# A transformer block on one core: new landing times, gates and priorities for the planner that orders its instructions

## The chip, the core and the metric

The kernel runs on one core of a Trainium2 chip. The core has five engines that each run their own instruction stream in order: TensorE (PE, matrix products; its weight loads are shown apart, as PEld), VectorE (DVE), ScalarE (ACT), GpSimd (POOL) and SyncE (SP, which here only issues DMA transfers). They wait for each other by semaphores. The metric is the device time of one execution in microseconds (us).

## What is computed

A block with 2048 rows of width 448: adaptive layer norm, a segment-wise attention with a compressive memory, adaptive layer norm, a gated FFN. Cut to what matters:

```python
mod = (silu(c) @ w_mod).reshape(1, 6, 1, 448)
sa, ca, ga, sb, cb, gb = (mod[:, i] for i in range(6))
h = layernorm(x) * (1 + ca) + sa
x = x + ga * A(h)            # attention
h = layernorm(x) * (1 + cb) + sb
x = x + gb * B(h)            # FFN: (sigmoid(h @ w_gate) * (h @ w_up)) @ w_down
# A: 16 heads of 28, 4 segments of 512 rows, in each segment s:
logits = q_s @ k_s.T * scale + causal mask
a_dot = softmax(logits) @ v_s
a_mem = (phi(q_s) @ M) / (phi(q_s) @ z + 1e-6)
o_s = g * a_mem + (1 - g) * a_dot     # g = sigmoid(beta), a number for each head
M, z = M + phi(k_s).T @ v_s, z + phi(k_s).sum()   # phi(t) = t + 1 if t > 0 else exp(t)
# then o @ wo
```

## The kernel before

The work is cut into four segments of 512 rows (four tiles of 128). A segment goes through these steps, each a function in the code:

- `ln1`: statistics (L607, L608) and scaling (L620, DVE, result xn), the power for the standard deviation on POOL (L614, L615), then turning to hT, features on partitions. Segments 0 to 2 turn in PE with an identity (`turned`, L821), segment 3 by a DMA transpose (`transposed`, L766, on SP). The turned tiles are scaled and shifted by the modulation columns `cols` while they are copied out of PSUM (L841 on DVE, L843 on ACT).
- `proj`: q, k and v (L881, L893) and their copies (L864, L866). The heads are taken in four groups; the weights wq and wk are first copied into a padded tile wqk (L696, the pads `W_p`).
- `attention`: logits (L962), exponential (L976, L982), causal mask (L989 on POOL, L992 on DVE), product with v (L1017), the memory's part (L1032), and a normalisation with 32 x 32 transposes on DVE (L1044 to L1069).
- `memory`: the update of M, with a DMA transpose pk (L917) and a product (L925).
- `wo_ln2`: output projection (L1084), residual (L1087), the second norm. Here the turning is by DMA transposes for all segments, and two DMA exchanges between the partition halves follow (`modulated`, L783 and L786).
- `ffn`: gate and up products (L1106), tanh (L1111), their product (L1113), the down projection (L1125), residual (L1132) and the store (L1134).

The modulation columns of the first norm come from two blocks of 32 small products (`mod_cols`, L659), which need w_mod, loaded in two halves into the tile pT by ACT's and SP's queues (`load_wm`). Each block is copied to `cols` (L671, L669). Warm-up products on zeros (L703) fill PE before the first data.

None of this is issued in program order. Each step adds a node to a graph, with a duration for each engine that may run it, dependences, buffers, a lag and a priority. `Graph.run` simulates the graph and fixes each engine's order for good: at each point of planned time an engine takes, among its ready nodes, the one with the highest rank plus priority. The rank is the length of the longest chain behind the node, in ns. The priorities come from the lists in PRM by kind of work and segment (`pr`), except for the prologue, which has fixed ones in units of BIG = 1e7. `COST` weighs the engines against each other where a node may run on several; `STAY` is a bonus for staying in one mode of PE. Where the plan leaves PE free for 465 ns or more, `fillers` puts in products on the identity (L1149), one for each 215 ns. The chip then runs this order, and waits wherever the plan was too hopeful.

A transfer's planned landing is the end of its bytes on a modelled link, plus 800 ns, plus its own lag. The lag is 300 for a load unless given, LATE for the first w_mod load. The bytes of a queue go at 215 per ns when it is alone and 111 when the other queue is busy too:

```python
a = max(self.ring[e], t)
b = self.ring["ACT" if e == "SP" else "SP"]
both = min(max(b - a, 0.0), size / SHARED)
self.ring[e] = a + both + (size - both * SHARED) / ALONE
```

Loads are kept from piling up: from load number UNTIED on, each waits for the third load ahead of it (`tie = loads[-DEPTH]`, L478 issues them). The loads in order are x tiles 0 and 1, c, x tiles 2 and 3, two halves of w_mod, wq, wk, x of segment 1 in two, wv in two, and then all others.

The fixed priorities of the prologue: turning of segment 0 and copies out, 2 BIG; modulation blocks, 1.5 BIG; pads, BIG.

Of the kernel before, what the change touches and what calls it, by code (L numbers as in the profile page):

```python
# [25 lines left out]
    "ld": (651902, 891758, 992046, 193839, 837972, 665983, 316786, 476619, 43274, 343803, 286986, 160628, 711024,  # L26
        773136, 92427, 200204, 1044173, 736930, 1243772, 692528, 937636, 616944, 1210630, 537419, 680585, -894676,
        101351, 728950, 607455, 1023026, 727687, 781942, 744416, 1320064, 1621173, 1242993, 1028480, 145604),
    "ws": (-134299, -217321, -175544, -243931, 15607, -528928, -1120744, 499755, -1822165, -1211957, -825377, -739006,
        -1049662, -916501, -1040707, -866299, -901616, -1444816),  # L30
    "pj": (2135341, 1765591, 2105194, 1672348, 1755362, 2254245, 1789709, 1512327, 2053089, 2138977, 2019869, 1835313,
        1733495, 1561732, 1467880, 1624953, 2164447, 1911795, 2076941, 1474725, 1071842, 2337649, 857487, 1479601,
        340869, -293016, -359807, -247015, -176478, -354654, -81637, -1181532, -1278023, -1553286, -1474034, -1392027,
        -2227875, -2649473, 738263, -485647, 458907, 1008596, 310603, 72906, -72493),
    "ev": (-294718, -287247, 213078, 345921, 516457, 617525, 581324, 337607, 190516, 201212, 1078717, 752663, -206309,
        -398653, -811894, 100457, 154660, -509455, -370130, -33664, 711493, 754309, 1092631, 1295115, 103302, -75744,
        -184717, 157515, -78688, 1103999, -567928, -409370, -842817, 129441, -1343027, -1834626, -1457093, -912663,
        -759990, -1105822, -1876991, -2484939, -1306058, -1489059, -1970976, -2040367, -2466205, -1875557),
    "ln1": (110333, -435438, 43989, 509127, 558340, 18640, -99722, 403841, 461985, -125721, 570633, 547192, 181038,
        589914, 838716, 388754, 1549344, 884134, 773881, 472463, 684753, 1450874, 1288325, -324762, -757540, 462703,  # L40
        235067, -196974, -90708, 130840, -2467, 24163, -173465, 12535, 560453, 321271, 141093, -574140, 352985,
        535548, -27157, 188824, 69165, 444536, -98687, 179524, -418944, -519050, -477785, -435607, 170856, 3212,
        -130603, 225709, -490768, -1222499, -1370121, -708993, -934798, -2273487, -922214, -1803841, -1194051,
        -1317455, -631182),
    "lg": (1930058, 1751837, 2089657, 1566292, 1503804, 777354, 1687163, 1461078, 820009, 478679, -574235, 441736,
        833992, 1205983, 71857, -209236, 98120, 699703, -386863, -451811, 1247966, 1710428, 1838855, 1608378, 1427664,
        1416671, 1472264, 1000048, 1902810, 635876, 2045809, 2348474, 1639360, 1253914, 1989642, 1870767, 1290318,
        1369680, 1105828, 441201),
    "ex": (820874, 1464092, 742402, 1721040, 1588269, 1846081, 2243894, 1771657, 1278231, 1694284, 1696793, 1148671,
        1565931, 874544, 290916, 2057927, 1431436, 2197370, 1532130, 1893428, 1169769, 1278223, 1429592, 1653293,  # L50
        1950929, 2335322, 1322958, 1489306, 651480, 1429262, -822129, -568907, -867507, -821319, -915357, -596973,
        -1379940, 58334, -1027319, -1394623),
    "mask": (871790, 1336268, 1642602, 1644196, 1580291, 1182991, 674167, 1522842, 1002934, 1339526, 1073208, 582064,
        806458, -167410, 381420, 458481, 768451, 1021063, 768364, 1088419, 901901, -33154, 1426954, 633166, 1054260,
        1617974, 575398, 1050025, 603812, 1402523, 831035, 1969148, -693227, -381531, 32884, 993657, 1101369, 762326,
        770126, 972849, 917495, 580251, 1626792, 824996, 833044, 991639, 1289478, 1708424, 1923893, 200297, 1240980,
        2126685, 1325623, 360160, 807428, 463327, 872714, 1369800, 930140, 1251419, 959998, 1315368, 1685662,
        1707343),
    "pv": (915183, 562989, -255863, 207624, -948513, -1784647, -1359691, -1851218, -448878, -576520, -1377485,
        -1039085, 451562, 1234285, 626677, 1171067),  # L60
    "t": (1504447, 1142971, 1498285, 249197, 2006853, 932728, 1830786, 1496977, 1797028, 1067225, 1669551, 1012448,
        1493008, 245545, 653293, 1730310, 1032521, 637393, 578213, 475817, 1194895, 670368, 1005069, 539542, 266975,
        1086409, 757943, -119979, 184266, 68176, 1299326, 1062841, 604854, 457056, 1415477, 944850, 1237728, 1143919,
        1252723, 678851, 1173350, 1767221, 1154668, 1170984, 1681291, 1120494, 1331949, 1053049, 114568, -116665,
        371052, 1074348, 157535, -270325, 57161, 181528, 155732, 83145, 820449, -137672, 478795, 592777, 337533,
        433694, -202781, -202925, -14119, -255487, 286501, -610255, -386903, -587025, -682549, -752560, -331807,
        -514855, 2993984, 2444729, 2526547, 2592569, 1889775, 2716625, 2740846, 2238225, 3066811, 2555029, 2940307,
        2968972, 3148894, 2939222, 3361905, 3605619, 3121992, 2896025, 3786564, 3061300, 4197354, 3108144, 3332194,
        2584841, 3453168, 2446031, 3115253, 2130779),
    "mem": (632660, 14836, 625612, 169379, -203457, 219971, 3166, -112832, -111979, 400067, 34302, -305861, -473627,  # L70
        724682, 1011534, 7776, -63822, -68838, -464677, 74183, -156399, -503372, 638892, 144364, 142364, 963326,
        143123, 722786, -135667, -577822, -742004, -540413, -835757, -207903, -673805, -93199, -145891, -144444,
        -1396541, -396310, -711511, -1297484, -612133, -706851, -521833, -164102, -1061841, -381836, -535280, -768057,
        -430175, -185845, -301056, -257799, -994564, -326051, 482086, -300754, 239236, -952235, 494754, -511897,
        -79917, -1085942, -464958, -54359, -490405, -912243, -220855, -554793, -1096452, -558009, -125262, -737088,
        -493049, 283968, -306712, -164819, -867118, -745049, -658321, -1182633, -704357, -75582),
    "wo": (-61225, -75610, -121003, -877351, 538559, 801450, 680069, 475534, 1947394, 2116079, 1713439, 2519473,
        1964361, 2559016, 1811544, 1942394),
    "ln2": (1346281, 1522029, 2339337, 1896659, 1268025, 1827698, 1561458, 2411495, 2740913, 2397362, 2049726,
        1098393, 2056240, 1643426, 1469752, 1516714, 1503039, 1478138, 884620, 2154157, 536839, 1153782, 1227142,  # L80
        1747539, 996154, 665586, 897788, 2523183, 1944058, 2236027, 1719000, 2079467, 2506460, 3182459, 1815723,
        2991530, 2290986, 2230887, 2272823, 2833817, 1237511, 2266504, 1938033, 2625708, 2553773, 1994448, 2041106,
        2451926, 2874528, 2571820, 2619831, 2092098, 966660, 1097378, 1524106, 456777, 1624191, 588984, 45196,
        1118750, 557760, -281000, 1006893, 656336, 1046263, 431849, 954219, 585672, 353355, -238055, 107673, 50010,
        345968, 893779, -98119, 643221, 921020, 288029, -1423125, -1558137, -1804997, -1640448, -1713062, -1930084,
        -1748829, -1453154, -1463181, -1412064, -2530358, -2348000, -2087770, -2284133, -2265972, -2613909, -2444750,
        -2567702, -2676544, -3771402, -2534665, -3238719, -1971814, -3299744, -2935510, -3033738),
    "gu": (354734, -15197, 452284, 727077, -177490, 490389, 991533, 1098033, 722194, 573386, 345008, -153917, 637103,
        553581, 563006, 683739, 596089, 885873, 850342, 930801, 510761, 1699749, 1022095, 1497866, 1021360, 753752,
# [23 lines left out]
        -742516, -2205172, -701131, -944493, -341370, -1186633, -855811, -1182823, -459652, -1152001, -584859),  # L113
}
STAY = 96324
COST = {"ACT": 0.957, "DVE": 0.883, "POOL": 0.756}


class Slot:
# [225 lines left out]
def kernel(  # L345
# [24 lines left out]
    NK = 4  # L370
# [100 lines left out]
    BIG = 1e7  # L471
# [36 lines left out]
    def first(i):  # L508
        return 5 * BIG - i * 1e6
# [673 lines left out]
```

## Time and profile before

| | us |
|---|---|
| median of 3 runs (lowest, highest) | 264.01 (263.14, 265.35) |
| profiled execution | 263.85 |
| its span, first to last instruction | 262.1 |
| PE busy in the span, fillers included | 245.5 |
| fillers (L1149) alone | 11.1 |
| DVE busy | 198.3 |
| ACT busy | 152.5 |
| POOL busy | 43.1 |

A span begins with the first instruction and ends with the last; the time of the execution has something around it. An engine's busy time is the sum of its instructions, so a PE that is busy may be busy with fillers, or at half clock: the mean granted clock of PE is 0.987 of full speed. A line of the timeline has the start, the duration of the instructions that were merged into it, engine and line of the code, the tiles, the number of instructions, and in brackets how long the engine was idle before and what ended that.

### The profile page before, as it was taken

How to read it: one execution, taken by the hardware profiler on the slowest of the kernel's cores; microseconds unless marked ns; L12 is line 12 of the kernel's file. 1: busy time of each engine (PE TensorE's matmuls, PEld its weight loads, DVE VectorE, ACT ScalarE, POOL GpSimd, SP SyncE). 2: the span in 40 equal slices, each digit the busy share in tenths (PEclk: the TensorE clock that was granted, in tenths of full speed). 3: DMA queues.
4: the chain of work that ended last, by engine and by line, in shares of the span. 5: the costliest groups of instructions: out<-in, count | busy, mean ns of one | idle time of the engine just before them, and what ended most of it. 6: DMA issues, size and time to landing. Idle time of an engine off the chain costs nothing.

```text
span 262.1 us, 6080 instructions
## 1 busy us (share of the span) xinstructions
PE 245.5 (94%) x2424; PEld 111.9 (43%) x2424; DVE 198.3 (76%) x497; ACT 152.5 (58%) x189; POOL 43.1 (16%) x99
## 2 busy tenths in 40 slices
PE   8799999789978999998999999999999999999994
PEld 3464545443333544443544344444344344454442
DVE  4749999987999999989499969898699754333431
ACT  5026989889987887663597745779730231122300
POOL 5205310010640224400000000503002200000000
PEclk9769999999999999999999999999999999999999
DMA  5975778997253200553111200132100420110011
GB/s 142 203 174 135 193 208 191 165 216 198 41 85 90 41 34 0 42 105 67 22 23 42 54 18 3 21 63 77 48 0 18 83 70 3 36 35 3 0 38 35
DMA packets 30088, 19.79 MB, mean 75 GB/s; under 512 B 18603, under 2 KB 28524, under 8 KB 30060
## 3 DMA queue, kind: packets, MB, share of 16 engines
q1 hardware_dynamic: 29532, 18.77, 32.8%
q10 hardware_dynamic: 528, 0.63, 0.9%
q8 instruction: 19, 0.31, 0.5%
q14 instruction: 9, 0.07, 0.1%
HBM read 11.07 MB, written 1.84 MB: 49 GB/s over the span
## 4 chain that ended last, share of the span: by engine, by line
PE 44%; DVE 29%; DMA 19%; issue 3%; ACT 2%; SPq 1%; POOL 1%; DVEq 0%; POOLq 0%; ACTq 0%
PE ps L1106 26%; PE ps L1125 10%; DMA wgu<-in_B_w_up_dram 4%; DMA pT<-in_w_mod_dram 3%; DVE x_sb L1087 3%; DVE st L607 3%; DMA hT<-hT 3%; DVE fT L1113 2%; DVE pT L992 2%; DMA fT<-in_w_mod_dram 2%; DVE A L1044 2%; PE ps L881 2%; DVE U L1059 2%; PE ps L1017 2%; PE ps L821 2%
## 5 line engine op out<-in xcount | busy, mean ns | idle before, releaser
L1106 PE MATMUL ps<-hT,wgu 64*128 64x512 bf16 x784 | 92.9, 377 | 2.6 <-DMA hT<-hT 1.4
L1111 ACT ACTIVATE tt<-ps 128x512 f32<-128x512 f32 x56 | 33.4, 596 | 60.5 <-PE ps L1106 54.4
L976 ACT ACTIVATE pT<-ps 128x2048 bf16<-128x2048 f32 x32 | 60.3, 1883 | 9.2 <-PE ps L962 8.7
L1106 PEld LDWEIGHTS <-wgu 64*128 64x128 bf16 x784 | 39.7, 94 | 49.3 <-issue 13.3
L1113 DVE SCALAR_TENSOR_TENSOR fT<-tt,ps 128x512 bf16<-128x512 f32 x56 | 37.9, 680 | 27.1 <-ACT tt L1111 27.1
L1125 PE MATMUL ps<-wd_sb,fT 128*128 128x448 bf16 x224 | 46.4, 354 | 0.2 <-DVE ot L1132 0.2
L1125 PEld LDWEIGHTS <-fT 128*128 128x128 bf16 x224 | 20.2, 98 | 22.8 <-issue 6.1
L881 PE MATMUL ps<-hT,wqk 64*128 64x512 bf16 x224 | 27.2, 377 | 0.3 <-DVE qT L866 0.3
L607 DVE BATCH_NORM_STATS2 st<-x_sb 128x6 f32<-128x448 bf16 x32 | 19.8, 618 | 3.1 <-DMA x_sb<-in_A_x_dram 2.8
L989 POOL TENSOR_SCALAR_AFFINE_SELECT pT<-pT 128x512 bf16<-128x512 bf16 x19 | 11.9, 636 | 58.3 <-ACT pT L976 28.9
L614 POOL TENSOR_SCALAR rs<-mv 128x1 f32<-128x1 f32 (+1 forms) x29 | 6.5, 225 | 81.3 <-DVE mv L608 52.8
L992 DVE TENSOR_TENSOR pT<-pT,cmask 128x512 bf16<-128x512 bf16 x45 | 17.4, 417 | 2.9 <-ACT pT L976 2.1
L615 POOL TENSOR_TENSOR rs<-rs,mhalf 128x1 f32<-128x1 f32 (+1 forms) x29 | 17.2, 594 | 2.4
L1132 DVE TENSOR_TENSOR ot<-ps,x_sb 128x448 bf16<-128x448 f32 x16 | 9.8, 617 | 9.0 <-PE ps L1125 8.7
L881 PEld LDWEIGHTS <-wqk 64*128 64x128 bf16 x224 | 11.0, 94 | 13.1 <-issue 2.2
L962 PE MATMUL ps<-qT,kT 28*128 28x512 bf16 (+3 forms) x256 | 15.9, 300 | 0.7 <-ACT pT L976 0.5
L982 ACT ACTIVATE pT<-ps 128x2048 bf16<-128x2048 f32 x8 | 15.1, 1881 | 1.6 <-PE ps L962 1.5
L1084 PE MATMUL ps<-wo_sb,oT 128*128 128x448 bf16 x64 | 13.5, 354 | 0.4 <-DVE oT L1069 0.4
L620 DVE TENSOR_SCALAR xn<-x_sb,mv,rs 128x448 bf16<-128x448 bf16 x32 | 11.4, 387 | 2.5 <-POOL rs L615 2.5
L1017 PE MATMUL ps<-pT,vt 128*32 128x512 bf16 (+3 forms) x256 | 11.4, 301 | 1.2 <-DVE pT L992 0.9
L893 PE MATMUL ps<-wvv,hT 64*128 64x448 bf16 x112 | 11.3, 350 | 0.0
L843 ACT ACTIVATE hT<-ps,cols 128x512 bf16<-128x512 bf16 x5 | 4.0, 800 | 12.3 <-DVE cols L669 10.9
(96 smaller groups left out, 260.1 us busy)
## 6 DMA issues: line engine op xcount, KB each, us to landing
out_dram<-ot SPq DMA_DIRECT2D x16, 112.0 KB, 1.7
fT<-in_w_mod_dram SPq DMA_DIRECT2D x8, 196.0 KB, 2.8
wgu<-in_B_w_gate_dram SPq DMA_DIRECT2D x7, 224.0 KB, 3.3
wgu<-in_B_w_up_dram SPq DMA_DIRECT2D x7, 224.0 KB, 3.6
wd_sb<-in_B_w_down_dram SPq DMA_DIRECT2D x7, 224.0 KB, 2.8
x_sb<-in_A_x_dram SPq DMA_DIRECT2D x6, 224.0 KB, 3.8
hT<-hT SPq DMA_DIRECT2D x5, 256.0 KB, 3.2
hT<-hT SPq DMA_DIRECT2D x5, 192.0 KB
```

The source lines that it names most:

```text
L607: nc.vector.bn_stats(st_r[:, st.at, :], src)
L615: nc.gpsimd.tensor_tensor(r, r, mhalf[:, 0:w], ALU.pow)
L881: nc.tensor.matmul(pf(b), lhsT=w, rhs=piece(hT, i, half), start=(i == 0), stop=(i == NP - 1))
L962: nc.tensor.matmul(ps[:, lg.at + hs, o:o + nq], lhsT=kT_r[r, k.at, hcs[u], kb * P:(kb + 1) * P], rhs=qT_r[r, q.at, hcs[u], kb * P:L], star ...
L976: nc.scalar.activation(pT_r[:, pTs[units[0]].at, :, w0:w0 + L], ps_, AF.Exp, scale=scale)
L982: nc.scalar.activation(dst, ps_.rearrange("p h (u w) -> p u h w", u=2), AF.Exp, scale=scale)
L992: nc.vector.tensor_tensor(blk, blk, cmask[:].rearrange("p (o k) -> p o k", o=1).to_broadcast([P, 4, P]), ALU.mult)
L1017: nc.tensor.matmul(pf(acc)[hs * HP:(hs + 1) * HP, kb * P:L], lhsT=vt_r[:, v.at, kb, hc * 4 + hs, :], rhs=pT_r[:, pT.at, hs, OFF[kb]:OFF[kb ...
L1106: nc.tensor.matmul(pf(b), lhsT=wgu[half * HR:(half + 1) * HR, chunk_of(i, half), fs], rhs=piece(hT, i, half), start=(i == 0), stop=(i == N ...
L1111: a = act(485, lambda gp=gp, tt=tt: nc.scalar.activation(tt_r[:, tt.at, :], pf(gp), AF.Tanh, scale=0.5), [n], use=[gp, tt], prio=pr("tanh" ...
L1113: f = dve(597, lambda up=up, tt=tt, ft=ft: nc.vector.scalar_tensor_tensor(fT_r[:, ft.at, :], tt_r[:, tt.at, :], 1.0, pf(up), op0=ALU.add, ...
L1125: nc.tensor.matmul(pf(b)[:, 0:D], lhsT=fT_r[:, fts[fc].at, t * P:(t + 1) * P], rhs=wd_sb[:, fc, :], start=(fc == 0), stop=(fc == NFC - 1))
```

## The change

Five things are changed, all in what the planner is told; no instruction is added or removed apart from fillers.

1. All priorities in PRM, and STAY and COST, have new values.
2. LATE, the lag of the first w_mod load, is 2200 instead of 500. wq and wk have lags of 1900 and 1200 instead of 900 each.
3. UNTIED is 13 instead of 9.
4. The pads of head group 0 have priority 2.5 BIG; the other groups keep BIG.
5. DMA transposes have a lag of 400 instead of 0; the two exchanges 900 and 1000 instead of 400 and 500.

```diff
-    "lg": (1930058, 1751837, 2089657, 1566292, 1503804, 777354, 1687163, 1461078, 820009, 478679, -574235, 441736,
...
+    "lg": (3531987, 2928887, 3302070, 2312646, 1981257, 2222351, 1556422, 2079865, 2540545, 1674238, 496386, 1265056,
...
-STAY = 96324
-COST = {"ACT": 0.957, "DVE": 0.883, "POOL": 0.756}
+STAY = 69838
+COST = {"ACT": 0.956, "DVE": 0.949, "POOL": 0.819}
...
-    EARLY, LATE = -900, 500
-    DEPTH, UNTIED = 3, 9
+    EARLY, LATE = -900, 2200
+    DEPTH, UNTIED = 3, 13
...
-    W_qk = [load_half("SP", wqk_st, half, w, first(6 + half), lag=900) for half, w in enumerate((A_wq, A_wk))]
+    W_qk = [load_half("SP", wqk_st, half, w, first(6 + half), lag=1900 - 700 * half) for half, w in enumerate((A_wq, A_wk))]
...
-            W_p.append(add(("DVE", "ACT", "POOL"), (415, 838, 830), pad, [W_qk[half], n_pads, n_th, *ln0], prio=BIG, lock=True))
+            W_p.append(add(("DVE", "ACT", "POOL"), (415, 838, 830), pad, [W_qk[half], n_pads, n_th, *ln0], prio=BIG if h else 2.5 * BIG, lock=True))
...
-        return add("SP", 1305, fn, [n], use=[xn, hT], prio=prio, move=60000)
+        return add("SP", 1305, fn, [n], use=[xn, hT], prio=prio, move=60000, lag=400)
...
-        xs = [add("SP", 530, below, hs[0:NK - 1], use=[hT], prio=prio(), move=80000, lag=400),
-              add("SP", 600, above, hs, use=[hT], prio=prio(), move=80000, lag=500)]
+        xs = [add("SP", 530, below, hs[0:NK - 1], use=[hT], prio=prio(), move=80000, lag=900),
+              add("SP", 600, above, hs, use=[hT], prio=prio(), move=80000, lag=1000)]
...
-                pk_r[:, pk.at, :, :], pq_r[:, f2.at, :]), [n], take=[pk], use=[f2], move=60000, prio=pr("mem", s))
+                pk_r[:, pk.at, :, :], pq_r[:, f2.at, :]), [n], take=[pk], use=[f2], move=60000, lag=400, prio=pr("mem", s))
```

The lists in PRM run over the segments; for the kinds that the prediction names, the mean of the quarter that belongs to a segment (millions, before and after):

| kind | segment 0 | segment 1 | segment 2 | segment 3 |
|---|---|---|---|---|
| lg, logits | 1.41, 2.41 | 0.17, 0.71 | 1.43, 0.90 | 1.54, 0.71 |
| t, normalisation | 1.07, 1.54 | 0.88, 0.24 | 0.16, 0.86 | 2.94, -0.69 |
| wo | -0.28, 1.80 | 0.62, 1.46 | 2.07, 0.47 | 2.07, 0.05 |
| ln2 | 1.60, 1.46 | 2.26, 1.01 | 0.60, -1.42 | -2.26, 2.51 |
| gu, gate and up | 0.48, 2.44 | 0.97, 0.44 | 0.62, 0.40 | 0.24, 0.71 |

## The prediction

> **What bounds the kernel now.** I read first the busy time in stretches of 20 us, then the prologue in the timeline, then the clock, then what TensorE (PE) waited for. Columns of the stretches: length, busy time of PE, its weight loads, VectorE (DVE), ScalarE (ACT), POOL, granted clock, DMA share, GB/s.
>
> ```profile
> 0.00:20.00 20.00, 16.84 (x135) 9.10 (x137) 10.92 (x36) 5.32 (x13) 5.25 (x23) 0.83 0.80 174
> 20.00:40.00 20.00, 19.46 (x232) 9.29 (x231) 19.12 (x57) 16.86 (x22) 7.45 (x18) 1.00 0.68 178
> 40.00:60.00 20.00, 17.55 (x268) 8.52 (x270) 17.80 (x57) 17.54 (x22) 1.28 (x2) 1.00 0.99 194
> 60.00:80.00 20.00, 17.23 (x168) 6.91 (x164) 18.31 (x47) 18.19 (x18) 7.61 (x14) 1.00 0.48 100
> 80.00:100.00 20.00, 19.53 (x219) 9.01 (x220) 19.48 (x48) 15.44 (x17) 4.58 (x7) 1.00 0.19 48
> ```
>
> PE looks full, but part of it is filler (L1149). The same stretches for that line alone, columns PE and weight loads:
>
> ```profile
> 0.00:20.00 20.00, 3.91 (x15) 1.45 (x15) 0.83 0.80 174
> 60.00:80.00 20.00, 4.75 (x18) 1.51 (x18) 1.00 0.48 100
> 80.00:100.00 20.00, 1.64 (x6) 0.50 (x6) 1.00 0.19 48
> ```
>
> So PE has three regimes. Up to 20 us it does almost nothing that counts; from 40 to 100 us it is starved (idle 2.45 + 2.77 + 0.47, fillers 4.75 + 1.64: 12.1 us), because DVE (89 to 97% busy) and ACT (77 to 91%) feed it; after 100 us it is the bound, idle 7.1 us in 162. The FFN's first product (L1106) starts only at 80.9 us. The prologue, in the timeline:
>
> ```profile
> 7.57 0.70 DVE L620 TENSOR_SCALAR xn<-x_sb,mv,rs 128x448 bf16<-128x448 bf16 x2
> 8.73 0.70 DVE L620 TENSOR_SCALAR xn<-x_sb,mv,rs 128x448 bf16<-128x448 bf16 x2 [0.46 <-POOL rs L615]
> 10.00 1.51 PE L659 MATMUL ps<-silu,pT 112*128 112x32 bf16 x32 [1.88 <-DMA pT<-in_w_mod_dram]
> 11.35 4.16 PE L821 MATMUL ps<-ident,xn 128*128 128x128 bf16 x32
> 15.30 1.30 PE L659 MATMUL ps<-silu,pT 112*128 112x32 bf16 x32
> 16.44 3.53 PE L1149 MATMUL ps<-ident 128*128 128x512 bf16 x14
> 16.84 2.35 DVE L841 TENSOR_SCALAR hT<-ps,cols 128x512 bf16<-128x512 bf16 x5
> 19.91 3.20 PE L881 MATMUL ps<-hT,wqk 64*128 64x512 bf16 x28
> ```
>
> The normalised tiles are there at 8.3 and 9.4 us, PE is free at 8.1, yet the 32 transposes (L821) stand behind the first modulation columns (L659), which wait for w_mod until 10.3; the second columns stand behind the transposes, and the first projection behind all of it, at 19.9. The clock is halved meanwhile (column after POOL):
>
> ```profile
> 8.00:10.00 2.00, 0.12 (x1) 0.00 (x1) 1.41 (x4) 0.00 (x0) 0.61 (x2) 1.00 1.13 201
> 12.00:14.00 2.00, 2.00 (x18) 1.38 (x16) 1.35 (x9) 0.00 (x0) 0.00 (x0) 0.50 0.96 208
> 16.00:18.00 2.00, 2.00 (x25) 1.05 (x22) 1.32 (x4) 0.78 (x1) 0.00 (x0) 0.70 0.97 214
> ```
>
> **The change: the order in the prologue.** LATE 500 to 2200 moves the planned landing of w_mod. By the code's own link arithmetic (start 2000, 215 or 111 bytes per ns, +800, +lag) its second half lands at 7.4 us planned before and at 9.1 after; the first tile's transposes are ready at about 7.5. I use the plan only for order: before, columns first; after, all four tiles first (2e7 outranks 1.5e7). On the chip: PE free at 8.13; tile 0 (8.13 to 8.62), tile 1 to 9.11, tile 2 when its xn is done (9.08, plus 0.1) to 9.67, tile 3 to 10.16. I took 61 ns for a transpose, from the later group that took 1.96 us for 32 at clock 1.00. The columns then start when w_mod is there, 10.29. Before, the first block's successor started 1.06 us after 10.29, and from the second block's start to the first hT copy were 1.54 us (15.30 to 16.84). So second block at 11.35, first copy at 12.89: **3.95 us earlier**.
>
> [...] In the trace it fell at 10.4, 2.2 us after the last dense product; by this row the moved transposes still run at full clock. If they were cold from the start, 32 would take the 4.16 us of the row, 8.13 to 12.29, and the first copy would be at 12.29 + 1.06 + 1.54 = 14.9: gain 1.95. I take 3.95, since the clock row at 8 to 10 us shows 1.00, and 1.9 as the other end.
>
> **The pads, and the loads behind them.** Pad copies of head group 0 (L696) get 2.5e7 and go ahead of the hT copies. wq landed before 12.1 (four pads ran at 12.12); wk, by when SP's tied issue went on, about 13.8. With lags 1900 and 1200 the plan puts the k pad behind the first hT copy; on DVE it then waits from 13.4 to 13.8 and takes 0.37, and four hT copies stand behind it, ACT taking the other two or three. Copies ended 2.8 us after their start before (16.84 to 19.62); after: 12.89 + 2.8 + 0.8 = 16.5 against 19.6. Without cover, each us that wk is late is a us for the copies. Projection of groups 0 and 1 is 28 instructions in 3.20 us; group 0 goes chunk by chunk behind the copies and ends near 16.9, group 1 near 18.5, against 23.1: gain 4.6. With the clock halved until 17.2 (as now) it ends near 19.3: 3.8; halved throughout, 20.0: 3.1. Fewer fillers (about 6 by the new gap instead of 14) make that end possible.
>
> UNTIED 13 lets four more loads go untied: x of segment 1 (two, 0.4 us of issue each) and wv (two, 0.61 and 1.33). On SP they pass its waits for w_mod (6.1 us), wq (0.9) and wk (1.7), and are issued from about 4 to 7 us; nothing else is on SP until the transposes at 40 us, POOL's queue issues none, and ACT's load isn't passed. They stand behind wk on the same queue, so wk shouldn't suffer; the hole in DMA at 14 to 16 us (53 GB/s there) goes, about 1.4 us of the load stream. wv landed 6.9 us after issue at 14.55, about 21.4; its product starts at 26.8, so it stays covered at 23.
>
> I take **3.5** for the prologue (ends 1.9 and 4.6).
>
> **Does it carry?** DVE is 45% idle before 20 us and nearly full behind it, and what feeds PE up to 80.9 is DVE and ACT work that can start 3.5 us sooner. Then it reaches the end: the last copy starts 3.3 us before the end and that is fixed.
>
> **The later landings.** Lags of 400 on DMA transposes and 900 and 1000 on exchanges put planned landings at 2.8 and 2.6 us or so, where the trace has 3.4 (pk), 2.9 and 3.2. What PE lost to these:
>
> ```profile
> PE ps L925 <- DMA pk<-pq: 2.9, 4, 1.0
> PE ps L659 <- DMA pT<-in_w_mod_dram: 1.9, 1, 1.9
> PE ps L1106 <- DMA hT<-hT: 1.4, 2, 0.9
> ```
>
> At most 4.3 us; at the pk waits PE is starved anyhow, so I count 0 (0 to 2).
>
> **All priorities, COST and STAY are new**, so everything behind the prologue is reordered too. No row prices this. From above: half the 12.1 us of holes (6). From below: 8 us, worked out under the rivals. I take 0: total work is unchanged and both old and new plans fill PE by the same rules.
>
> Sum: 262.1 - 3.5 = 258.6 us of span; the profiled execution took 263.85, 1.75 more than its span, so 260.35; it lay 0.16 under the median: **260.5 us**.
>
> **Rivals.**
> 1. *Load stream binds (no change).* DVE waits 1.36 us for w_down at 60.8, the end of the stream. If such waits set the pace, only the 1.4 us hole is gained, 262.6. For: DMA share 0.99 from 40 to 60 us, and the chain runs through loads from 22 to 41. Against: w_down isn't used before 130.8, and loads make only that one DVE wait there.
> 2. *The last segment comes late (slower).* The new lists raise the first segment's FFN (gu mean 0.48 to 2.44 million) and lower the last segment's attention (lg 1.54 to 0.71, t 2.94 to -0.69), while its ln2 rises from -2.26 to 2.51. PE then does FFN early and attention of segment 3 slips. An FFN needs about 33.7 us of PE (196 instructions of L1106 at 28 in 3.13 us: 21.9; 56 of L1125 at 5 in 1.05: 11.8), plus 3.4 of tail. Now segment 3's opens near 216 us; for a span of 258.6 it must open by 221.5, and every us later costs one. From 227.6 it is 1% slower than before; at 230, 269. For: DVE is 90% busy from 20 to 180 us, so what slips isn't caught up. Against: 5 us of slack, and DVE only 35% busy after 220.
> 3. *More: FFN opens early.* The same lists (wo of segment 0 from -0.28 to 1.80) open the first FFN before 80.9; half of the 60 to 80 us hole (7.5) filled gives 3.7 more: 256.8.
> 4. *The change doesn't act:* transposes still behind the columns, prologue as now: 264.
>
> **Chances.** Likeliest, prologue carried: 0.50 (own range 258 to 262.5). Load stream or no action, 262 to 265: 0.16. Slower by mechanism 2, 265.5 to 270: 0.23. More: 0.11. Faster by over 1% (under 261.4; 1% is about what a measurement of this kernel tells from no change): 0.11 + 0.41 = 0.52. Slower (over 266.6): 0.20. Within: 0.28. The range 256 to 267.5 leaves out some 5 below and 14 above in a hundred.
>
> **What would show it.** L821 in one block from about 8.1 us, ahead of both L659 blocks, which run together from 10.3; first hT copy near 12.9, first L881 near 14.3, its second group done by 19.3; wv issued before 8 us; PE waits for pk and hT under 2 us in sum. Carried: the first L1106 by 77.5. Wrong if the first copy is after 15, if wk's pad holds DVE past 15, if holes from 40 to 100 exceed 12.1 us, or if the last segment's FFN opens after 221.5.

## The result, and the profile after

| | before | after |
|---|---|---|
| median (lowest to highest), 20 executions each, us | 263.81 (261.36 to 266.12) | 262.79 (260.42 to 267.02) |
| ratio after / before | | 0.9961 [0.9938, 0.9984] |
| profiled execution, us | 263.85 | 261.97 |
| its span, us, and mean granted clock | 262.1, 0.987 | 260.3, 0.985 |
| PE busy, fillers among it, us | 245.5, 11.1 | 241.0, 3.9 |

The change brings about 1.0 us; forecast were 3.5. The number is that of rival 1 (262.6). Ratios here and below leave out executions more than 1.5% above the fastest of their own kernel (two of the 20 after), while medians and ranges have them all.

The prologue does what the prediction says. The timeline of PE, and the first copies on DVE, after:

```profile
7.99 2.63 PE L821 MATMUL ps<-ident,xn 128*128 128x128 bf16 x32
10.46 2.04 PE L659 MATMUL ps<-silu,pT 112*128 112x32 bf16 x64
12.35 1.24 PE L1149 MATMUL ps<-ident 128*128 128x512 bf16 x5
13.52 1.30 PE L881 MATMUL ps<-hT,wqk 64*128 64x512 bf16 x6
15.29 2.57 PE L881 MATMUL ps<-hT,wqk 64*128 64x512 bf16 x22 [0.47 <-ACT hT L843]
```

```profile
12.54 0.17 DVE L669 TENSOR_SCALAR cols<-ps 128x7 f32<-128x7 f32 x1 [0.19 <-PE ps L659]
12.74 0.54 DVE L841 TENSOR_SCALAR hT<-ps,cols 128x512 bf16<-128x512 bf16 x1
13.40 0.39 DVE L696 COPY wqk<-wd_sb 64x784 bf16<-64x784 bf16 x1
13.82 1.45 DVE L841 TENSOR_SCALAR hT<-ps,cols 128x512 bf16<-128x512 bf16 x3
```

The transposes stand in one block ahead of both column blocks, the first hT copy is at 12.74 instead of 16.84, and both first groups are projected at 17.86 instead of 23.1. The k pad (13.40) waits for nothing. The clock, halved from 10.4 to 17.2 before, is whole here:

```profile
12.00:14.00 2.00, 2.00 (x26) 0.89 (x21) 1.63 (x6) 0.62 (x1) 0.00 (x0) 1.00 1.13 244
16.00:18.00 2.00, 2.00 (x22) 0.85 (x19) 1.88 (x5) 1.16 (x3) 0.00 (x0) 1.00 0.95 185
```

So over 5 us are won at 20 us, and of them 1.9 arrive at the end of this execution. The stretches of 20 us after (PE, weight loads, DVE, ACT, POOL, clock, DMA share, GB/s) show where to look:

```profile
0.00:20.00 20.00, 18.33 (x175) 9.33 (x177) 13.85 (x43) 9.15 (x18) 6.67 (x27) 1.00 0.89 189
20.00:40.00 20.00, 17.41 (x208) 7.75 (x203) 17.97 (x53) 17.43 (x20) 5.93 (x15) 0.91 0.66 178
40.00:60.00 20.00, 15.33 (x202) 7.26 (x199) 16.81 (x52) 14.73 (x19) 3.68 (x6) 0.91 0.80 180
60.00:80.00 20.00, 17.17 (x217) 7.05 (x217) 19.48 (x54) 17.12 (x20) 6.88 (x14) 1.00 0.37 90
80.00:100.00 20.00, 19.06 (x250) 8.38 (x251) 19.18 (x54) 14.35 (x19) 1.86 (x3) 1.00 0.19 40
```

From 20 to 60 us PE is busy for 32.7 us instead of 37.0, and the clock is at 0.91 where it was 1.00. What PE waited for:

```profile
PE ps L925 <- DMA pk<-pq: 5.0, 2, 4.3
PE ps L1106 <- DMA hT<-hT: 1.8, 2, 1.3
PE ps L881 <- DVE hT L841: 1.5, 1, 1.5
...
PE ps L679 <- DMA fT<-in_w_mod_dram: 1.0, 1, 1.0
```

and where, in its timeline:

```profile
26.70 1.02 PE L679 MATMUL ps<-fT,U 112*128 112x448 bf16 x4 [1.00 <-DMA fT<-in_w_mod_dram]
...
32.54 1.26 PE L881 MATMUL ps<-hT,wqk 64*128 64x512 bf16 x6 [1.51 <-DVE hT L841]
...
51.46 0.30 PE L925 MATMUL ps<-vt,pk 128*32 128x32 bf16 x16 [4.33 <-DMA pk<-pq]
```

At two of these waits the clock is halved for some 3.4 us, from 33.9 to 37.3, behind the wait at L881, and from 50.9 to 54.4, beginning in the wait for pk:

```profile
34.00:36.00 2.00, 2.00 (x24) 0.74 (x22) 1.67 (x5) 1.65 (x1) 1.26 (x3) 0.50 0.74 206
52.00:54.00 2.00, 2.00 (x14) 0.77 (x10) 0.88 (x4) 0.00 (x0) 0.00 (x0) 0.50 0.50 116
```

To follow the lead through two different orders I counted, in both traces, how much real PE work is done at a time (each product at its spacing in stretches at clock 1.00, some 112 ns for L1106, where 28 took 3.13 us from 101.55 to 104.68 after, and 61 for L821, where 32 took 1.96 us; without L1149 and L703), and took the time less that work. After minus before, in us (minus is a lead); this is an estimate, and some matmul records can be missing from a trace, so it is good to 1 or 2 us:

| at us | 20 | 30 | 40 | 55 | 95 | 160 | 255 |
|---|---|---|---|---|---|---|---|
| lead | -5.0 | -3.0 | -0.6 | +3.0 | -4.0 | -0.2 | -2.1 |

The lead of the prologue is gone at 40 us. What comes back by 95 is another thing: the new order opens the first FFN at 75.1 instead of 80.9 and fills the holes from 60 to 100 us with it (fillers there 0.60 us instead of 6.39). Much of that is lost again by 160; from 95 to 160 PE is idle for 3.9 us instead of 2.4, which is 1.5 us of it, and the rest isn't explained.

### The profile page after: what moved, and what is told of

It is laid out like the page before. It is cut to its first block, busy times and chain, and to the rows that moved or that the text cites. A ratio compares the mean times of both kernels' runs of the same rounds, so it can differ in the third digit from the quotient of the medians.

```text
span 260.3 us, 6026 instructions
## 1 busy us (share of the span) xinstructions
PE 241.0 (93%) x2397; PEld 107.0 (41%) x2397; DVE 197.4 (76%) x497; ACT 152.6 (59%) x189; POOL 42.6 (16%) x99
## 4 chain that ended last, share of the span: by engine, by line
PE 40%; DVE 12%; DMA 3%; issue 1%; POOL 1%; SPq 0%; DVEq 0%
PE ps L1106 23%; PE ps L1125 13%; PE ps L1084 2%; DMA pk<-pq 2%; DMA hT<-hT 1%; DVE fT L1113 1%; DVE aT L1040 1%; DVE x_sb L1087 1%; DVE U L1059 1%; DVE pq L909 1%; DVE A L1044 1%; DVE pT L992 1%; PE ps L1017 1%; DVE st L607 1%; DVE ot L1132 1%
## 5 line engine op out<-in xcount | busy, mean ns | idle before, releaser
L1106 PE MATMUL ps<-hT,wgu 64*128 64x512 bf16 x784 | 92.3, 377 | 2.5 <-DMA hT<-hT 1.8
L1106 PEld LDWEIGHTS <-wgu 64*128 64x128 bf16 x784 | 39.0, 94 | 48.9 <-issue 12.5
L881 PE MATMUL ps<-hT,wqk 64*128 64x512 bf16 x224 | 28.8, 386 | 2.4 <-DVE hT L841 1.5
L989 POOL TENSOR_SCALAR_AFFINE_SELECT pT<-pT 128x512 bf16<-128x512 bf16 x23 | 14.5, 638 | 92.8 <-DVE pT L992 22.2
L881 PEld LDWEIGHTS <-wqk 64*128 64x128 bf16 x224 | 11.1, 95 | 16.5 <-issue 7.1
L615 POOL TENSOR_TENSOR rs<-rs,mhalf 128x1 f32<-128x1 f32 (+1 forms) x29 | 17.2, 591 | 2.4
L992 DVE TENSOR_TENSOR pT<-pT,cmask 128x512 bf16<-128x512 bf16 x41 | 16.1, 418 | 1.0 <-ACT pT L976 0.7
L893 PE MATMUL ps<-wvv,hT 64*128 64x448 bf16 x112 | 13.1, 378 | 0.0
L909 DVE TENSOR_TENSOR pq<-e 128x512 bf16<-128x512 bf16 x24 | 10.1, 423 | 4.0 <-ACT aT L864 2.1
L1017 PE MATMUL ps<-pT,vt 128*32 128x512 bf16 (+3 forms) x256 | 12.2, 312 | 0.0
```

Source lines behind the costliest of these rows:

```text
L615: nc.gpsimd.tensor_tensor(r, r, mhalf[:, 0:w], ALU.pow)
L881: nc.tensor.matmul(pf(b), lhsT=w, rhs=piece(hT, i, half), start=(i == 0), stop=(i == NP - 1))
L992: nc.vector.tensor_tensor(blk, blk, cmask[:].rearrange("p (o k) -> p o k", o=1).to_broadcast([P, 4, P]), ALU.mult)
L1106: nc.tensor.matmul(pf(b), lhsT=wgu[half * HR:(half + 1) * HR, chunk_of(i, half), fs], rhs=piece(hT, i, half), start=(i == 0), stop=(i == N ...
```

## The experiments

"Lead" below compares two kernels that issue the same instructions: the start of the same instruction in one trace less that in the other, so minus is earlier.

**Turning first, alone.** Before, with only the first column block moved:

```diff
+    pe.remove(block)
+    pe.insert(pe.index(turn[-1]) + 1, block)
```

> The kernel before, with one thing moved: on TensorE the four turning groups (L821) stand ahead of the first modulation block (L659); every other order is as it was. Theory A (a lead won in the prologue is carried, and what the change lost was lost later, at late transposes, halved clock and in the new order): the first hT copy about 3.5 us sooner, and the end 2.5 to 3.5 us sooner, ratio to before 0.987 to 0.991. Theory B (something behind the prologue, the load stream or VectorE, sets the pace and swallows any lead): the first copy just as early, the end within 1 us of before, ratio 0.996 to 1.000.

Measured: 263.24 us, ratio 0.9995 [0.9976, 1.0014]. Lead of PE: 4.5 us at 20, 3.3 at 36, 1.7 at 40, 0.1 at 44, 0.6 at the end. The timeline shows the place; first before, then this kernel:

```profile
38.42 0.69 PE L659 MATMUL ps<-silu,fT 112*128 112x32 bf16 x16
...
39.55 0.68 PE L659 MATMUL ps<-silu,fT 112*128 112x32 bf16 x16
40.16 1.69 PE L881 MATMUL ps<-hT,wqk 64*128 64x512 bf16 x14
```

```profile
35.15 0.19 PE L659 MATMUL ps<-silu,fT 112*128 112x32 bf16 x1
35.90 0.21 PE L659 MATMUL ps<-silu,fT 112*128 112x32 bf16 x2 [0.56 <-DMA fT<-in_w_mod_dram]
36.91 0.62 PE L659 MATMUL ps<-silu,fT 112*128 112x32 bf16 x13 [0.80 <-DMA fT<-in_w_mod_dram]
...
38.42 2.93 PE L881 MATMUL ps<-hT,wqk 64*128 64x512 bf16 x14
```

PE comes 3.3 us early to two parts of w_mod that land only 0.4 us earlier (35.9 and 36.9 instead of 36.3 and 37.2) and waits for both, 0.56 and 0.80 us. Behind the waits the same 14 products take 2.93 us instead of 1.69, in a stretch at half clock (mean clock 0.68 from 38 to 40 us, where the profile of before has 1.00). No wait for loads stood in this place in the profile of before, because PE came late enough.

**The reverse.** After, with the first block put back ahead of turning: `pe.insert(pe.index(turn[0]), block)`.

> The changed kernel, with the first modulation block (L659) put back ahead of the four turning groups on TensorE; every other order is that of the changed kernel. Theory A: the first hT copy 3.5 to 4 us later than in the changed kernel (16.5 instead of 12.7 us), and the end 2.5 to 4 us later, ratio to before 1.005 to 1.011. Theory B: the end at most 1 us later than the changed kernel, ratio 0.996 to 1.000.

Measured: 263.99 us, ratio 0.9996 [0.997, 1.0023], where the changed kernel has 0.9961: by the ratios some 0.9 us are lost. Here L821 x32 takes 2.63 us with the old order, and the first copies are only 1.3 us later than after. That was the first sign that the 4.16 us of the profile of before were not a property of the order. Nor is the loss at the end the prologue's. PE is 1.2 us behind the changed kernel at 20 us, level at 26, 0.2 behind from 55 to 78, and 2.0 behind from 95: a wait for hT at 80 us is 0.3 us longer here (1.63), and the 21 products behind it take 4.03 us instead of 2.53. The changed kernel, too, swallows what its prologue loses or wins.

**Do waits need cover?** After, with 7 fillers ahead of segment 1's first projection and 16 ahead of the first L925: `fill[id(pk)] = (pk.take[0].at, 16)`, `fill[id(proj)] = (proj.take[0].at, 7)`.

> The changed kernel with 23 fillers more and nothing moved: 7 ahead of the first projection of segment 1 (where TensorE waited 1.5 us at 31 us) and 16 ahead of the first memory product L925 (where it waited 4.3 us at 47 us), written into the banks that those products take anyway. Theory A: the granted clock stays at 1.00 from 33 to 37 us and from 51 to 54 us, which takes 1.5 to 2.5 us of slow products away; of it 1 to 2 us reach the end, ratio to before 0.989 to 0.993. Theory B: the clock stays up, the end is that of the changed kernel, ratio 0.995 to 0.998.

Measured: 262.01 us, ratio 0.9955 [0.9932, 0.9977]. The fillers need a bank that the awaited copy itself releases, so they ran behind the wait (L1149 waited for hT, twice 1.8 us), and the trace is 1.4 to 1.8 us behind the changed kernel from 38 to 125 us. The mean clock rose all the same (ten of the 22 executions at 0.994 or more; of the changed kernel's 20 none is over 0.987), and by the ratios (0.9955 and 0.9961) the time is that of the changed kernel. Since the fillers cost time where they were to save some, this run doesn't say what the clock alone is worth.

**The longest wait.** After, with the first L925 two steps later on PE: `pe.insert(i + 2, pe.pop(i))`.

> The changed kernel with the first memory product (L925, which waited 4.3 us for the DMA transpose pk at 47 us) moved two steps back on TensorE, behind a v projection (L893) and a product with v (L1017); nothing else is moved. Theory A: the wait falls from 4.3 to about 2 us, the clock stays up at 51 us, and 1.5 to 3 us reach the end, ratio to before 0.985 to 0.991. Theory B: the wait goes, the end is that of the changed kernel, ratio 0.995 to 0.998.

Measured: 262.07 us, ratio 0.9945 [0.992, 0.9971]. The trace leads the changed kernel by 2.2 us from 60 to 75, and by 0.4 at 85. Changed kernel, then this one:

```profile
79.98 2.53 PE L1106 MATMUL ps<-hT,wgu 64*128 64x512 bf16 x21 [1.35 <-DMA hT<-hT]
```

```profile
78.13 4.00 PE L1106 MATMUL ps<-hT,wgu 64*128 64x512 bf16 x21 [1.73 <-DMA hT<-hT]
```

A little more wait (1.73 for 1.35) and slower products behind it (4.00 us for 2.53) take back 1.8 us. Here removing one wait moves the loss to the next transfer.

**Loads: a first try.** The kernel with turning first alone; in it the four w_mod loads for the second norm's columns are issued ahead of the loads that stood just before them on SP, still three in flight.

> The kernel before with the turning groups first (as in the first run of this study), and on SP the four loads of w_mod for the second norm's columns moved ahead of five loads of wgu and w_mod; the depth of three loads in flight is kept along the new order. Theory C (the lead is lost where the fixed order meets the load stream: TensorE waits for w_mod at 35 to 37 us, and the clock halves after it): the columns' block L659 doesn't wait, the clock stays at 1.00 from 38 to 42 us, a lead of 2 us or more is left at 44 us, and the end is 1 to 3 us sooner than before, ratio 0.989 to 0.996. Theory D (the lead is lost to the feeding engines, whatever the loads do): the lead is gone by 44 us again, ratio 0.998 to 1.001.

Measured: 266.66 us, ratio 1.0098 [1.0066, 1.013]: slower, against the forecast. PE's waits in this kernel:

```profile
PE ps L679 <- DMA fT<-in_w_mod_dram: 3.9, 1, 3.9
```

The load of the earlier user, L679, came later for it, and a lead of 2.5 us turned into 3.6 us lost at 36. With three in flight, one load ahead is another one late.

**Loads: five in flight.** No order is changed; from load 13 on each waits for the fifth load ahead, not the third:

```diff
+    if n.tie is not None and i >= 13:
+        n.tie = ld[i - 5]
```

With turning first, and before with nothing else changed:

> The kernel before with the turning groups first, and from load 13 on each load waits for the fifth load ahead of it instead of the third; no order is changed. Theory C: the load stream runs 2 to 3 us earlier at 36 us, the lead stays past 44 us, ratio 0.989 to 0.996, unless the DMA transposes pk (40 to 56 us) come later behind more loads in flight and give it back as waits of L925 (more than 1 us each). Theory D: loads earlier, end as before, 0.998 to 1.001.

> The kernel before with five loads in flight instead of three from load 13 on, and nothing else: the transposes stand behind the first modulation block. Theory C (a lead in the prologue is swallowed where the fixed order meets the load stream; deeper loading alone has no lead to save): the end within 1 us of before, ratio 0.996 to 1.001. Theory E (the load stream by itself set the pace, the prologue doesn't matter): as fast as with both, ratio 0.984 to 0.989.

Measured: 260.52 us, ratio 0.9851 [0.9815, 0.9888], and 261.59 us, ratio 0.9866 [0.9815, 0.9917]. The second is the number of theory E, loads alone, but it spreads with the clock: three of its six executions had 0.999 or more (258.35 to 260.66 us), three 0.987 or less (262.52 to 263.96). The last runs take this up. With turning first the lead is 3.7 us at 20, 2.8 at 40, 3.0 at 255: it reaches the end. The stretches from 24 to 28 and 36 to 40 us, with three in flight (the first experiment), then with five (columns as above: clock, DMA share, GB/s last):

```profile
24.00:28.00 4.00, 4.00 (x59) 2.56 (x56) 3.93 (x12) 3.91 (x6) 1.58 (x5) 1.00 0.68 163
...
36.00:40.00 4.00, 3.20 (x45) 1.83 (x46) 2.52 (x12) 2.67 (x4) 0.43 (x1) 0.84 0.71 201
```

```profile
24.00:28.00 4.00, 4.00 (x59) 2.97 (x55) 3.97 (x11) 4.00 (x5) 2.02 (x5) 1.00 0.97 219
...
36.00:40.00 4.00, 3.90 (x66) 2.05 (x64) 3.93 (x17) 4.00 (x7) 0.64 (x1) 1.00 0.95 190
```

The DMA engines weren't full at 0.68; with looser ties they reach 0.97. The two loads that PE waited for at 35.9 and 36.9 landed at 34.6 and 35.6, and the L659 waits are gone:

```profile
35.60 0.69 PE L659 MATMUL ps<-silu,fT 112*128 112x32 bf16 x16
...
37.33 1.69 PE L881 MATMUL ps<-hT,wqk 64*128 64x512 bf16 x14
```

**Five in flight in the changed kernel,** and with the first L925 later as well:

> The changed kernel with five loads in flight instead of three from load 13 on, no order changed. By theory C its wait for w_mod (L679, 1.0 us at 26 us) goes and 1 to 2.5 us more of the prologue's lead reach the end, ratio to before 0.987 to 0.993; the wait for pk at 47 us (4.3 us) stays or grows by up to 1 us, as it stands behind more loads. By theory F (the loss of the changed kernel is its own order in the middle, not the loads) the end is that of the changed kernel, 0.994 to 0.998.

> The changed kernel with five loads in flight and the first memory product (L925) two steps later on TensorE. By theory C this adds both repairs: a lead of 3 us or more over the kernel before at 60 us, ratio 0.983 to 0.990. By theory F 0.992 to 0.997.

Measured: 260.04 us, ratio 0.9884 [0.9848, 0.9919], and 260.82 us, ratio 0.9899 [0.9873, 0.9925]; L925 later adds nothing that the intervals could tell. The first is the lowest median of all kernels here, though not the lowest ratio. Its PE timeline at the places of the changed kernel's waits:

```profile
26.44 0.92 PE L679 MATMUL ps<-fT,U 112*128 112x448 bf16 x4
...
32.86 1.26 PE L881 MATMUL ps<-hT,wqk 64*128 64x512 bf16 x6 [1.77 <-DVE hT L841]
...
48.48 0.27 PE L925 MATMUL ps<-vt,pk 128*32 128x32 bf16 x16 [2.36 <-DMA pk<-pq]
```

and SP's queue, in the changed kernel, then here:

```profile
45.30 0.47 SPq L478 DMA_DIRECT2D wgu<-in_B_w_gate_dram  x1
45.81 1.30 SPq L917 DMA_TRANSPOSE pk<-pq  x1
```

```profile
44.29 1.29 SPq L917 DMA_TRANSPOSE pk<-pq  x1
```

In the changed kernel pq is ready at 45.0 (L909) and the transpose goes out 0.8 us later, behind a load that waits for its tie, and PE goes on 5.65 us after the issue; with five in flight the issue comes 0.04 us after pq and PE goes on 4.2 us after it. The clock from 20 to 40 us is 1.00 instead of 0.91; from 40 to 60 it is 0.91 in both, the halved stretch behind the wait for pk stays, and so does the wait at L881, which is DVE's: not every loss is the loads'.

**UNTIED, undone.** After, with loads 9 to 12 tied on the chip as before, the order kept: `loads[9].tie, ..., loads[12].tie = loads[6:10]`.

> The changed kernel, with loads 9 to 12 (x of segment 1, wv) waiting on the chip for the third load ahead of them as in the kernel before; the planned order is kept. The first projections of segment 0 don't need these loads; x of segment 1 comes some us later (issued from 10 us instead of 4.4), and the load stream has its hole at 14 us back (1.4 us). By theory C 0.5 to 1.5 us slower than the changed kernel, ratio 0.998 to 1.002; if untied loads don't matter, 0.995 to 0.998.

Measured: 263.00 us, ratio 1.0005 [0.9982, 1.0027]. Undoing this one edit takes the whole gain back, and so did undoing the order of the prologue (0.9996); the two don't add up to shares. In its timeline L679 waits twice:

```profile
27.08 0.54 PE L679 MATMUL ps<-fT,U 112*128 112x448 bf16 x2 [1.10 <-DMA fT<-in_w_mod_dram]
28.53 0.54 PE L679 MATMUL ps<-fT,U 112*128 112x448 bf16 x2 [0.91 <-DMA fT<-in_w_mod_dram]
```

That is 2.0 us of waits instead of 1.0; the four loads that went out early had pulled the two parts of w_mod for L679 forward by 0.4 and 1.3 us.

**Lists and landings apart.** Each half of the planner's new input, the rest as the other kernel has it, planned anew: lists, STAY and COST alone; then all else alone.

> The kernel before with the new priority lists, COST and STAY alone; landing times, UNTIED and the pads' priority are the old ones. If the small gain of the change comes from its order behind the prologue, this has it (ratio to before 0.994 to 0.998) although the transposes stand behind the modulation block again; if it comes from the prologue, this is no faster than before (1.000 to 1.006). A list that was made for other landing times may also do worse than either (up to 1.02).

> The kernel before with the new landing times, UNTIED and the pads' priority alone; lists, COST and STAY are the old ones, so the planner makes a third order. The prologue should run as in the changed kernel (first hT copy near 12.8 us). By what the first four runs showed (a lead of 4 us in the prologue was gone by 44 us) I expect little of it at the end: ratio 0.997 to 1.005. If the prologue were worth what I predicted it would be 0.985 to 0.990.

Measured: 313.47 us, ratio 1.1838 [1.178, 1.1897], and 272.80 us, ratio 1.0318 [1.0273, 1.0364]. The priorities fit only the landings with which they were found; a plan with half of the change is another program, and these two runs say nothing on how the gain divides.

**Order or clock?** Before, with nine fillers instead of one in the hole ahead of the first column block (they write the block's own bank, which is free): `fill[id(block)] = (fill[id(block)][0], 9)`. The order stays that of before. With three and with five in flight:

> The kernel before, its order untouched, with nine filler products (L1149) instead of one ahead of the first L659 block, in the stretch from 8 to 10 us in which PE waits for w_mod. Theory 1 (of the 3.95 us that the prediction gave to turning first, some 2.6 are the clock that was halved in the one profiled execution of before, and the order itself is worth 1.3): L821 x32 takes about 2.6 us, not 4.16, the first hT copy is at 14.0 to 14.5 us, and the time falls by no more than 1 us, 262.3 to 263.3, because the loads behind w_mod bind next. Rival (the order is what counts, the clock follows from it): L821 still takes about 4 us and the first copy stays at 16.8.

> The kernel before with the same nine fillers and, from load 13 on, each load tied to the fifth ahead instead of the third; the order of the prologue stays that of before (columns first). Theory 1: with loads no longer binding, the prologue counts, but 2.6 of its 3.95 us were clock; so this kernel is within 0.7 us of the one that turns first with five in flight (about 260.5), at 260.2 to 261.2. Rival (the order itself carries): it stays 1.3 us or more above it, 262 or more.

Measured: 263.03 us, ratio 0.9991 [0.9969, 1.0013], and 260.63 us, ratio 0.9887 [0.9848, 0.9927]. The timeline of the first:

```profile
6.71 2.10 PE L1149 MATMUL ps<-ident 128*128 128x512 bf16 x9
9.67 1.28 PE L659 MATMUL ps<-silu,pT 112*128 112x32 bf16 x32 [0.85 <-DMA pT<-in_w_mod_dram]
10.79 2.63 PE L821 MATMUL ps<-ident,xn 128*128 128x128 bf16 x32
```

The old order with the clock held takes 2.63 us, as turning first does; its first hT copy is at 14.60. It has a lead of 2.6 us at 20 and loses it from 36 to 50, with three in flight: 0.45 us in waits of L659 for w_mod, 2.40 in a wait for pk, whose transposes stand between the loads in SP's queue, and half clock behind it (mean clock 0.91 from 40 to 60 us). With five it keeps 3.0 at 140 and 3.3 at the end. So it reaches, without the new order, what turning first reaches.

**Both once more.** Five in flight with turning first, and with the columns first and no fillers:

> The kernel before with turning first and five loads in flight, once more, for an interval beside the two kernels that keep the columns first. Theory 1 (turning first holds the clock through the prologue, and with five in flight the lead lasts): nearly every run has a mean granted clock of 0.998 or more, median 260.5. Rival (the fast median of the first five runs was chance): a median of 261.5 to 262, as the old order with five in flight has it.

> The kernel before with five loads in flight, columns first, once more. Theory 1: its runs fall into two groups by the mean granted clock, about 260.5 us at 1.00 and about 263 at 0.98 to 0.99, because here the clock is halved in the prologue in some executions and not in others; the median lies between, 261 to 262.5. Rival (five in flight alone gives the whole 3 us, turning first nothing): a median of 260.5, as with turning first.

Measured: 260.87 us, ratio 0.9873 [0.9826, 0.992], and 262.92 us over 19 executions, ratio 0.9909 [0.9882, 0.9936] over eleven of them. The two ratios can't be told apart; the clocks can. With turning first, of the twelve executions of its two runs one is under 0.992 of mean clock (0.987, 263.64 us), and all others are at or under 261.73 us. With the columns first, all 19 executions go by the number of stretches at half clock, which I estimate from the mean clock (3.4 us at 0.50 take 0.0065 off the mean over 260 us): none (0.997 or more), seven, median 261.03 us; one, three, 262.36; two, four, 263.56; three, five, 264.89. Of the two theories the one in which the clock scatters fits.

Two profiled executions of this one program, columns first with five in flight, show where it scatters; first that of the earlier run, then that of this one (whose view ends at 21 us, within the fillers):

```profile
10.43 2.63 PE L821 MATMUL ps<-ident,xn 128*128 128x128 bf16 x32
...
13.84 3.18 PE L1149 MATMUL ps<-ident 128*128 128x512 bf16 x14
```

```profile
11.22 4.16 PE L821 MATMUL ps<-ident,xn 128*128 128x128 bf16 x32
...
16.31 4.89 PE L1149 MATMUL ps<-ident 128*128 128x512 bf16 x13
```

In the second the clock is halved from 10.0 to 20.2 us (mean 0.75 from 0 to 20), in the first nowhere before the end (1.00 in all stretches of 20 us up to 160). Against before, PE is 2.9 us early at 20 us in the first and 1.4 late in the second; at 255 us it is 3.3 early and 1.0 late. With five in flight what the prologue wins or loses reaches the end, and in the execution without an early prologue five in flight alone gained nothing.

## Why the prediction was wrong

**The order in the prologue: right in the trace, wrong as a worth of the order.** Forecast were 3.95 us for the first copy; the two profiled executions differ by 4.10. But of this some 2.6 us are the clock of one execution. The old order was seen with L821 x32 in 2.63 us in four profiles (the changed kernel with the block first, the first of before with five in flight, before with fillers twice), and the first copies then were 1.3 to 1.9 us behind those of the changed kernel. I took the row of one execution for what the order costs. The mean clock of other executions, measured since, shows how far it stands for them: the profiled execution had 0.987, two stretches of 3.4 us (10.4 to 17.2 us), and by the same estimate from the mean clock, of the 71 executions of before in the first experiment's ratio 3 had none (median 262.51 us), 42 one (262.73), 23 two (263.74) and 3 three (264.36). Why the clock is halved there in one execution and not in another, no run shows. For the other end, 1.9, all 32 transposes were put at half clock, 4.16 us; no profile with the transposes first shows that. After, they took 2.63 us, and the clock stayed at 1.00 from 0 to 20 us; so it did in the old order once the clock was held up to them (2.63 us again, 1.00 from 0 to 20).

**Pads and loads: right in the main.** The projection ends at 17.86, ahead of the forecast 18.5 to 19.3, and the k pad costs no wait. The first half of wv goes out at 6.02, the second only at 9.04 (forecast for both: before 8). UNTIED was put at 1.4 us of load stream; undoing it costs 1.1 us at the end, by the ratios.

**The failed step is "Does it carry?"** "[...] what feeds PE up to 80.9 is DVE and ACT work that can start 3.5 us sooner. Then it reaches the end." The work does start sooner, but it is fed by loads that don't: with three in flight their pace is set by their landings, and with turning first SP issues them only 0.2 to 1.6 us earlier (10 to 40 us). The prologue's lead shrinks where PE meets the next load, L679 at 26 us in the changed kernel and L659 at 35 in the old order, and such a wait came with about as much again in clock: with turning first 1.36 us of waits at L659, and behind them 14 products that took 1.24 us longer. In the changed kernel the 4.4 us that are lost from 20 to 40 us are 1.0 at L679, 1.5 at L881, which waits for DVE and not for a load, and about 1.7 in the stretch at half clock; then comes the wait of 4.3 for pk. That loads in flight decide over the lead is shown twice: two ways to the same early start (turning first, clock held) both come to nothing with three (0.9995, 0.9991), and both carry with five (0.9851 and 0.9873; 0.9887). The ratio of five in flight alone (0.9866, 0.9909) would not exclude that the loads do it all; its two profiles speak against it, since in them the end follows the prologue. The changed kernel itself goes from 0.9961 to 0.9884 with five, some 2.0 us.

I had rejected rival 1, that the loads set the pace, because the profile shows one wait for a load in 60 us. That profile shows which wait is last with PE late; it doesn't show how far behind the next one is. That distance was to be had: the start of each load's user less its landing is slack, and at the L659 of 38.4 us it was some 2.1 and 1.3 us (landings at 36.3 and 37.2), less than the 3.5 that I carried past it. That rival 1 also has the number (262.6) is in part luck: it knew nothing of the waits for pk and DVE and of the clock. And my sign for a carried lead, the first L1106 by 77.5, came (75.1) and told nothing, since the new order alone can open the FFN early.

**Later landings, at 0.** PE's waits for pk and hT rose from 4.3 to 6.8 us, and under 2 were forecast. A planned lag of 400 puts pk some 2.8 us after the issue, while PE went on 5.65 us after the first. The longest wait is worth something (2.2 us at 60 us without it), but in that run the next transfer took most of it back.

**Reordering, at 0.** By the estimate above PE is 4.0 us ahead at 95 and 0.2 at 160; segment 3's FFN opens at 219.97, ahead of the 221.5 of rival 2, which did not come. Rival 3's early opening came (75.1 us), and no gain like its 3.7 us shows at the end. How much of the final 1.0 us is owed to the lists stays open, since the lists can't be run without the landings.

By executions with equal clock the changed kernel is better than its median: 261.74 us where two stretches were halved (ten executions) against 263.74 before. But by its mean clock (0.987 or less) it had two or more in every execution, where before mostly had one or two. That its waits cause this is argued from the places of the two halved stretches; no run took away both waits and nothing else.

## What to carry to other kernels

A stage that gets ready earlier gains no more than the slack of the transfers that it meets next, if these don't move with it; so list first use less landing for each of them before a lead is carried to the end (here 2.1 and 1.3 us at L659, against a lead of 3.5), and lengthen the queue of loads if the DMA engines have room (here a share of 0.68 from 24 to 28 us with three in flight, 0.97 with five). A stretch at half clock in one profile needn't be a cost of the code at that place (the same 32 transposes in the same order took 4.16 us in one execution and 2.63 in another): set the mean granted clock of the profile against that of the other runs first. Here a wait that was cut moved to the next transfer (L925 later: 1.73 us at hT instead of 1.35); five loads in flight instead of three moved the end by 2.0 to 3.8 us where the prologue was early.

## What was unexpected of the hardware

In these traces stretches at half clock began in a short wait or soon behind it, but not behind each. PE was idle for 1.51 us at L881 after, up to 32.54, and a stretch at 0.50 began at 33.88, 1.3 us later; the wait for pk was 4.33 us, up to 51.46, and a stretch began within it, at 50.94. The two last 3.41 us each and begin 17.06 us apart. With turning first the idle times at L659 were 0.56 and 0.80 us, and the clock went down some 1.8 us behind the second, at about 38.7 (0.68 from 38 to 40 us). With L925 later, 21 products of L1106 took 4.00 us instead of 2.53 behind a wait of 1.73. But a wait of 1.35 us was followed by none (L1106 after, 1.00 from 80 to 100 us), nor was one of 1.77 us (L881 with five in flight, 1.00 from 33 to 36). What decides on it, no run shows. And loads of 98 to 224 KB, three in flight, kept the DMA engines busy for 0.47 to 0.74 of the time from 20 to 36 us with turning first; five took them to 0.63 to 0.99.
